# DeltaNet and SwiGLU FFN: diagonal blocks by substitution on VectorE, chunks in two half steps, output product behind each h tile

## The chip, the core and the metric

The kernel runs on one core of a Trainium2 chip. The metric is the device time of one execution in microseconds (us): 1305.42 as the median of three runs (1304.56 to 1309.9). The engines are TensorE (PE; PEld is its weight load), VectorE (DVE), ScalarE (ACT), GpSimd (POOL) and SyncE (SP), which issues the DMAs.

## What is computed

Four sequences of 768 tokens with 8 heads of width 48 go through a delta rule; its output, 3072 tokens of width 384, goes through a SwiGLU FFN of width 1536 behind an RMS norm. All is fp32; the FFN weights come as float64 and are converted in the kernel.

```python
k_n = k / (np.linalg.norm(k, axis=-1, keepdims=True) + 1e-06)
for t in range(S):
    y[:, :, t] = np.einsum('bhd,bhde->bhe', q[:, :, t], state)
    v_old = np.einsum('bhde,bhd->bhe', state, kt)
    state = state + bt[:, :, :, None] * np.einsum('bhd,bhe->bhde', kt, vt - v_old)
...
rms = np.sqrt(np.mean(x * x, axis=-1, keepdims=True) + 1e-06)
xn = x / rms * rms_g
g = xn @ w_gate
silu = g * (1.0 / (1.0 + np.exp(-g)))
val = xn @ w_val
return (silu * val @ w_out).astype(np.float32)
```

## The kernel before

Each sequence is cut into 6 chunks of 128 tokens; a unit n is chunk c = n // 4 of sequence b = n % 4, 24 units in all, with all 8 heads of the sequence. Within a chunk the recurrence is a triangular system with unit diagonal: (I + lower part of beta K K^T) u = beta (v - K state).

`invert(n)` (L249) prepares a unit. It normalizes k (knrm, krec), makes beta k (kb) and beta v, transposes k, beta k and q on PE (p_t, L285), and multiplies keys by keys and queries (p_g, L301, 64x128 tiles for even and odd heads); masks give xn (32x32 blocks on the diagonal) and gq (L309). Five doubling levels (L321) invert the four 32x32 diagonal blocks of each head: p_q (L326) and p_m (L337) are 32 matmuls of 32x32 each, with ScalarE (qc) and VectorE (new, m, mt) between. Then come ne (the inverse as block diagonal, POOL L358), the off-diagonal product (p_a L371, off) and xn = -ne off (p_x L384).

`recur(n)` (L391) uses it: r = beta v - beta K state (p_b), z0 = inverse r (p_z), three Horner steps u = z0 + xn u (p_h, L417), the output p_y from state and u, the state update p_s, the RMS norm (ms, rs, y) and the transposed FFN input xt.

`ffn(m)` (L490) takes two units, 256 tokens: for 12 tiles f of the hidden width p_gv (gate and value, L498), sil on ScalarE and h_f on VectorE; all 12 h_f are kept, and then the output product p_o (L516) runs over them for each half of the tokens.

`weights()` (L183) converts the weights in 30 items: seven VectorE operations on the two words of each float64 and a product on POOL (L243). All gate and value items come ahead of the output weights.

Every engine works through its queue in order. The order in which work is recorded comes from a plan (L534): each generator has a start time and a step, and the one that is due next is taken. Invert, recur and ffn of neighbouring units are so laid into one another; the build then puts each engine's instructions into a fixed order.

## Time and profile before

| | us |
|---|---|
| median of three runs | 1305.4 |
| profiled execution | 1309.4 |
| its span, first to last instruction | 1307.6 |
| mean granted TensorE clock | 0.97 of full |
| first p_gv of the FFN | 189.7 |

The page gives an engine's busy time and share, 40 equal slices with a digit of tenths for each, and the chain of work that ended last by engine and line. A row of a group has line, engine, operation, output<-inputs, shapes and count; behind the bar its busy time in all, the mean of one in ns, the idle time of the engine ahead of it and what ended that. Timeline rows begin with start and length in us. In PE rows 64*128 stands for the rows and columns of the tile, and 128x256 behind it for the output.

### The profile page before, as it was taken

The numbers are of one execution on the slowest core, as the hardware profiler recorded it, in microseconds if no ns is written. First come the engines' busy times: TensorE is split into PE (matmuls) and PEld (weight loads), VectorE is DVE, ScalarE is ACT, GpSimd is POOL, SyncE is SP. The second block draws the span as 40 slices with busy tenths as digits, with TensorE's granted clock in tenths as the row PEclk, the third lists the DMA queues.
The fourth block names the chain that finished last, engine by engine and source line by source line (L and its number), as shares of the span: only waits on it lengthen the run. The fifth ranks groups of instructions, "written<-read, shape, count | busy, mean of one in ns | idle before, by whom it ended". The sixth has DMA issues, their size and how long they took to land.

```text
span 1307.6 us, 43286 instructions
## 1 busy us (share of the span) xinstructions
PE 1222.7 (94%) x20206; PEld 1006.6 (77%) x20206; DVE 528.5 (40%) x1290; ACT 225.4 (17%) x506; POOL 216.6 (17%) x182
## 2 busy tenths in 40 slices
PE   3367898999999999999999999999999999999999
PEld 2266877878878878968878868878878878878976
DVE  6999763423333324334334333333432432332210
ACT  1011121112212212212212112112112121111110
POOL 6343341101111111011011011111111110000000
PEclk9967598999999999999999999999999999999999
DMA  8343210001000000010010010010000000000000
GB/s 149 111 121 98 72 30 14 14 21 20 14 21 15 19 21 14 14 27 14 15 27 14 9 28 19 9 26 20 9 20 15 15 14 8 3 8 8 1 13 13
DMA packets 83283, 35.91 MB, mean 27 GB/s; under 512 B 76160, under 2 KB 79232, under 8 KB 83104
## 3 DMA queue, kind: packets, MB, share of 16 engines
q1 hardware_dynamic: 83104, 33.14, 10.6%
q8 instruction: 159, 2.61, 0.8%
q14 instruction: 20, 0.16, 0.0%
HBM read 28.41 MB, written 4.72 MB: 25 GB/s over the span
## 4 chain that ended last, share of the span: by engine, by line
PE 76%; DVE 6%; POOL 3%; DMA 0%; issue 0%; ACT 0%; SPq 0%
PE p_gv L498 28%; PE p_o L516 13%; PE p_h L417 8%; PE p_q L326 5%; PE p_m L337 4%; PE p_x L384 3%; PE p_y L433 3%; PE p_z L409 3%; PE p_t L285 2%; POOL knrm L265 2%; PE p_a L371 2%; DVE xn L309 2%; PE p_y L424 1%; PE p_b L399 1%; DVE gq L309 1%; PE p_s L445 1%
## 5 line engine op out<-in xcount | busy, mean ns | idle before, releaser
L498 PE MATMUL p_gv<-xt,wg_sb 128*128 128x256 f32 x864 | 219.3, 389 | 0.0
L498 PE MATMUL p_gv<-xt,wv_sb 128*128 128x256 f32 x864 | 218.9, 389 | 0.0
L516 PE MATMUL p_o<-wo_sb,h_f 128*128 128x384 f32 x576 | 204.4, 497 | 0.0
L498 PEld LDWEIGHTS p_gv<-xt,wv_sb 128*128 128x128 f32 x864 | 155.4, 190 | 22.4 <-issue 3.3
L498 PEld LDWEIGHTS p_gv<-xt,wg_sb 128*128 128x128 f32 x864 | 153.8, 190 | 21.5 <-issue 3.3
L510 DVE TENSOR_TENSOR h_f<-sil,p_gv 128x256 f32<-128x256 f32 x144 | 60.2, 418 | 245.4 <-ACT sil L508 245.4
L516 PEld LDWEIGHTS p_o<-wo_sb,h_f 128*128 128x128 f32 x576 | 103.5, 190 | 65.1 <-issue 6.6
L418 DVE TENSOR_TENSOR u<-z,p_h 128x384 f32<-128x384 f32 x72 | 39.9, 554 | 216.5 <-PE p_h L417 216.5
L508 ACT ACTIVATE sil<-p_gv 128x256 f32<-128x256 f32 x144 | 55.3, 384 | 363.7 <-PE p_gv L498 363.7
L358 POOL TENSOR_TENSOR ne<-mt,mask_blk 128x1024 f32<-128x1024 f32 x24 | 57.5, 2395 | 312.6 <-DVE mt L354 276.4
L326 PEld LDWEIGHTS p_q<-m,xn 32*32 32x32 f32 x6144 | 65.5, 110 | 55.9 <-issue 53.4
L337 PE MATMUL p_m<-qc,mt 32*32 32x32 f32 x6144 | 78.0, 200 | 24.9 <-DVE mt L354 12.7
L417 PEld LDWEIGHTS p_h<-u,xn 128*128 128x128 f32 x768 | 98.1, 203 | 2.8 <-DVE u L418 1.1
L417 PE MATMUL p_h<-u,xn 128*128 128x48 f32 x768 | 98.2, 283 | 0.9 <-DVE u L418 0.9
L326 PE MATMUL p_q<-m,xn 32*32 32x32 f32 x6144 | 76.1, 199 | 20.8 <-DVE m L347 20.8
L337 PEld LDWEIGHTS p_m<-qc,mt 32*32 32x32 f32 x6144 | 66.3, 111 | 35.7 <-issue 24.6
L331 ACT COPY qc<-p_q 128x256 f32<-128x256 f32 x96 | 35.8, 372 | 312.6 <-PE p_q L326 312.6
L341 DVE TENSOR_TENSOR new<-p_m,mask_lev 128x256 f32<-128x256 f32 x96 | 40.6, 423 | 102.5 <-PE p_m L337 95.8
L301 PE MATMUL p_g<-kbq,knt 64*128 64x256 f32 x384 | 63.9, 412 | 1.4 <-ACT kbq L288 1.4
L276 POOL TENSOR_TENSOR v_raw<-v_raw,beta_t 128x384 f32<-128x384 f32 x24 | 20.8, 867 | 253.2 <-DMA v_raw<-in_v_dram 253.1
L472 POOL TENSOR_TENSOR rs<-ms,mhalf 128x1 f32<-128x1 f32 x24 | 13.4, 558 | 291.2 <-DVE ms L470 291.2
L384 PEld LDWEIGHTS p_x<-ne,off 128*128 128x128 f32 x384 | 54.2, 206 | 6.6 <-POOL ne L358 4.2
(102 smaller groups left out, 1386.3 us busy)
## 6 DMA issues: line engine op xcount, KB each, us to landing
kpad<-in_k_dram SPq DMA_DIRECT2D x24, 192.0 KB, 2.8
qpad<-in_q_dram SPq DMA_DIRECT2D x24, 192.0 KB, 2.8
v_raw<-in_v_dram SPq DMA_DIRECT2D x24, 192.0 KB, 2.8
raw<-in_moe_w_gate_dram SPq DMA_DIRECT2D x9, 512.0 KB, 4.4
raw<-in_moe_w_val_dram SPq DMA_DIRECT2D x9, 512.0 KB, 3.5
raw<-in_moe_w_out_dram SPq DMA_DIRECT2D x12, 384.0 KB, 3.1
out_dram<-o_sb SPq DMA_DIRECT2D x24, 192.0 KB, 1.9
beta_sb<-in_beta_dram SPq DMA_DIRECT2D x1, 96.0 KB, 2.1
```

The lines of the kernel that those rows point to most:

```text
L301: nc.tensor.matmul(p_gs[par][:, jj].rearrange("p a t -> p (a t)"), knt[lo : lo + DP, j], kbq[lo : lo + DP, j].rearrange("p a t -> p (a t)"),)
L326: nc.tensor.matmul(p_q[w, h], abd[w, h, w], m[w, h] if lev else ident_c[w], skip_group_check=True)
L337: nc.tensor.matmul(p_m[w, h], mt[w, h], qc[w, h], skip_group_check=True)
L341: nc.vector.tensor_tensor(out=new, in0=p_m, in1=mask_lev[:, lev, None, :].to_broadcast([128, H, W]), op=ALU.mult,)
L358: nc.gpsimd.tensor_tensor(out=ne, in0=mt[:, :, None, :].to_broadcast([128, H, NBLK, W]), in1=mask_blk[:, None].to_broadcast([128, H, NBLK, ...
L384: nc.tensor.matmul(p_x[:, i], off[:, h], ne_f[:, h])
L417: nc.tensor.matmul(p_h[:, h], xn[:, h], (u if it else z0)[:, h])
L418: nc.vector.tensor_tensor(out=u, in0=z0, in1=p_h, op=ALU.add)
L498: nc.tensor.matmul(p_gv[:, i], w_sb[:, t, f * 128 : (f + 1) * 128], xt[:, t], start=(t == 0), stop=(t == KT - 1),)
L508: nc.scalar.activation(out=sil, in_=p_gv[:, 0], func=ACTF.Silu)
L510: nc.vector.tensor_tensor(out=h_f, in0=sil, in1=p_gv[:, 1], op=ALU.mult)
L516: nc.tensor.matmul(p_o, hs[f][:, i * C : (i + 1) * C], wo_sb[:, f], start=(f == 0), stop=(f == FT - 1),)
```

## The change

Work is now planned by cycles of four units, chunk c of all four sequences, with two FFN calls in each cycle. `prepare(n)` forms key by key and key by query products in 64x64 tiles without beta (kqt, gp; p_g moves 192 columns). `invert(c)` inverts the diagonal blocks of all four units at once on VectorE: 128 partitions hold 4 blocks of 32 rows, the free dimension 32 heads by 32 by 32; 31 substitution steps of two operations update ttb. `merge(n)` joins 32-row blocks to 64-row ones (p_v, p_w) and makes x2 (p_x), which couples the two halves. `recur(n)` solves the upper 64 rows (p_z, u[lo]) and then the lower (p_z second, u[hi]); beta is applied to u. `weights()` now has 36 items of 384 columns, ordered so that three f tiles have gate, value and output weights together; ScalarE does four of the steps, and POOL none. In `ffn` the output product of tile f - 1 follows the gate and value product of tile f, in two PSUM buffers of its own.

```diff
-LEVELS = 5
-HORNER = C // W - 1
+HC = 64
+K1, K0, Q0, Q1 = 0, 2, 3, 4
...
+def weights(dt):
...
+                nc.scalar.activation(
+                    out=exp_f, in_=exp, func=ACTF.Relu, scale=1.0, bias=lift[:, 1:2]
+                )
+                nc.scalar.activation(
+                    out=exp_f, in_=exp_f, func=ACTF.Relu, scale=-1.0, bias=lift[:, 2:3]
+                )
...
-                nc.gpsimd.tensor_tensor(out=dst, in0=dst, in1=exp.bitcast(FP32), op=ALU.mult)
+                nc.vector.tensor_tensor(out=dst, in0=dst, in1=exp_f, op=ALU.mult)
...
+def prepare(n):
...
+                for par, i in ((0, 0), (1, 1), (0, 1), (1, 0)):
+                    lo = slice(DP * par, DP * (par + 1))
+                    rhs = pair[lo, K1 : K1 + 5 : 2] if i else pair[lo, K0 : K0 + 3]
+                    nc.tensor.matmul(
+                        p_gs[par][HC * i : HC * (i + 1), jj].rearrange("p (a t) -> p a t", a=3),
+                        pair[lo, K1 if i else K0],
+                        rhs,
+                        skip_group_check=True,
+                    )
...
+def invert(c, dt):
...
+            nc.vector.transpose(
+                out=gblk[p], in_=gp_all[p, :, o : o + W].rearrange("p x j -> p j x")
+            )
...
+        for i in range(W - 1):
+            n = W - 1 - i
+            shape = [128, n, i + 1]
...
+            nc.vector.scalar_tensor_tensor(
+                out=tmp,
+                in0=gblk[:, i, i + 1 :, None].to_broadcast(shape),
+                scalar=nbeta[:, c, i : i + 1],
+                in1=ttb[:, i : i + 1, 0 : i + 1].to_broadcast(shape),
+                op0=ALU.mult,
+                op1=ALU.mult,
+            )
+            to = ttb[:, i + 1 :, 0 : i + 1]
+            nc.vector.tensor_tensor(out=to, in0=to, in1=tmp, op=ALU.add)
+            yield dt
+        nc.vector.transpose(out=back, in_=ttb)
...
+def recur(n, dt):
...
+        for h in range(H):
+            for p in (lo, hi):
+                nc.tensor.matmul(
+                    p_z[p, h], tt[b][p, h], r[p, h], start=(h == 0), stop=(p is lo), skip_group_check=True
+                )
+        nc.vector.tensor_tensor(out=u[lo], in0=p_z[lo], in1=over_d(lo), op=ALU.mult)
...
+            nc.tensor.matmul(
+                p_z[hi, h], x2[:, h], u[lo, h], start=False, stop=True, skip_group_check=True
+            )
+        nc.vector.tensor_tensor(out=u[hi], in0=p_z[hi], in1=over_d(hi), op=ALU.mult)
...
+        for h in range(H):
+            first = c == 0 and h == 0
+            nc.tensor.matmul(
+                p_y[lo, h], sc[lo, h, HC : 2 * HC], u[lo, h], start=first, stop=True, skip_group_check=True
+            )
+            nc.tensor.matmul(
+                p_y[hi, h], sc[:, h, 2 * HC : 3 * HC], u[:, h], start=first, stop=True, skip_group_check=True
+            )
...
 def ffn(m):
...
+            if last is not None:
+                leave(f - 1, last)
+                yield 1
+            last = h_f
...
+    CYC = 3 * FT * B // 2
+    at(-69, weights(2.1))
+    for c in range(NCH):
+        t0 = CYC * (c - 1)
+        for b in range(B):
+            n = B * c + b
+            at(t0 - 1 + 5 * b, prepare(n))
+            at(t0 + 46 + 0.6 * b, merge(n, 2.7))
+            at(t0 + 50.1 + 2.7 * b, recur(n, 3))
+        at(t0 + 25.3, invert(c, 0.55))
+        for g in range(B // 2):
+            at(CYC * c + CYC // 2 * g, ffn(B // 2 * c + g))
```

Three places of the order. First PE, around the output of a unit in the steady stage, before:

```order
L498 MATMUL p_gv<-xt,wv_sb 128x256 x3
L424 MATMUL p_y<-state_95,kbq 128x96 x4
L433 MATMUL p_y<-u,gq 128x48 x8
L445 MATMUL p_s<-u,kpad_85 64x48 x8
L301 MATMUL p_g<-kbq,knt 128x256 x4
L516 MATMUL p_o<-wo_sb,h_f 128x384 x3
```

and of the change:

```order
L532 MATMUL p_gv<-xt,wg_sb 128x256 x3
L443 MATMUL p_s<-u,kpad_82 64x48 x8
L453 MATMUL p_y<-state_85,kqt_90 64x96 x8
L463 MATMUL p_y<-u,gp 64x48
L466 MATMUL p_y<-u,gp 64x48
L463 MATMUL p_y<-u,gp 64x48
L466 MATMUL p_y<-u,gp 64x48
```

The eight 128-row products of u became 16, in turn 64 rows (L463, upper half) and 128 rows (L466, lower half), one pair for each of the 8 heads (two pairs are shown).

Second VectorE, around the FFN's h_f, before:

```order
L341 TENSOR_TENSOR new<-p_m,mask_lev 128x256
L347 TENSOR_TENSOR m<-m,new 128x256
L354 STREAM_TRANSPOSE mt<-m 128x256
L510 TENSOR_TENSOR h_f<-sil,p_gv 128x256
L418 TENSOR_TENSOR u<-z_5648,p_h 128x384
```

and of the change, in the middle of the elimination (tmp and ttb are its product and its result):

```order
L543 TENSOR_TENSOR h_f<-sil,p_gv 128x256
L325 SCALAR_TENSOR_TENSOR tmp<-gblk,nbeta,ttb 128x156
L334 TENSOR_TENSOR ttb<-ttb,tmp 128x26x6
L325 SCALAR_TENSOR_TENSOR tmp<-gblk,nbeta,ttb 128x175
L334 TENSOR_TENSOR ttb<-ttb,tmp 128x25x7
L325 SCALAR_TENSOR_TENSOR tmp<-gblk,nbeta,ttb 128x192
L334 TENSOR_TENSOR ttb<-ttb,tmp 128x24x8
L325 SCALAR_TENSOR_TENSOR tmp<-gblk,nbeta,ttb 128x207
L334 TENSOR_TENSOR ttb<-ttb,tmp 128x23x9
L325 SCALAR_TENSOR_TENSOR tmp<-gblk,nbeta,ttb 128x220
L543 TENSOR_TENSOR h_f<-sil,p_gv 128x256
```

Between two h_f there now stand about nine operations of one dependent chain.

Third PE, where the first FFN call begins, before:

```order
L417 MATMUL p_h<-z_2081,xn 128x48 x6
L326 MATMUL p_q<-ident_c,xn 32x32 x12
L498 MATMUL p_gv<-xt,wg_sb 128x256 x2
L498 MATMUL p_gv<-xt,wv_sb 128x256 x3
L498 MATMUL p_gv<-xt,wg_sb 128x256 x2
L326 MATMUL p_q<-m,xn 32x32 x32
```

and of the change:

```order
L463 MATMUL p_y<-u,gp 64x48
L466 MATMUL p_y<-u,gp 64x48
L504 MATMUL p_xt<-ident,y 128x128 x3
L532 MATMUL p_gv<-xt,wg_sb 128x256 x3
L532 MATMUL p_gv<-xt,wv_sb 128x256 x3
L504 MATMUL p_xt<-ident,y 128x128 x3
L266 MATMUL p_t<-ident,qpad_83 128x128 x4
```

The first FFN call now stands behind the products of u and the state update of all four units of chunk 0; before, it stood among Horner steps and block inversions of units that were still under way.

## The prediction

> **What bounds the kernel now.** The page comes first: busy shares, the 40 slices, and the chain that ended last.

> ```profile
> PE 1222.7 (94%) x20206; PEld 1006.6 (77%) x20206; DVE 528.5 (40%) x1290; ACT 225.4 (17%) x506; POOL 216.6 (17%) x182
> ...
> PE   3367898999999999999999999999999999999999
> ...
> PEclk9967598999999999999999999999999999999999
> ...
> PE 76%; DVE 6%; POOL 3%; DMA 0%; issue 0%; ACT 0%; SPq 0%
> ```

> TensorE (PE) is the bound in all but the first six slices (some 200 us). The table of stages gives the two parts apart (busy us of each engine, then the clock, the DMA share, GB/s).

> ```profile
> 0.00:50.00 50.00, 15.49 (x418) 12.50 (x418) 38.93 (x111) 5.78 (x10) 27.88 (x28) 1.00 0.68 139
> 50.00:100.00 50.00, 30.06 (x764) 26.54 (x754) 46.53 (x97) 5.30 (x11) 18.28 (x12) 0.75 0.40 114
> 100.00:150.00 50.00, 39.08 (x882) 35.20 (x883) 44.81 (x108) 6.60 (x15) 17.62 (x15) 0.67 0.33 93
> ...
> 500.00:600.00 100.00, 98.58 (x1687) 80.78 (x1686) 35.42 (x88) 18.27 (x41) 14.24 (x12) 1.00 0.08 18
> ```

> At first VectorE (DVE) is busy 45 of 50 us while it converts weights, and PE waits. Later PE works 98.6 of 100 us at full clock and DVE 35. Third, the chain in order of time (start, length, what) gives the period.

> ```profile
> 189.74 1.80 PE p_gv L498 x4
> ...
> 424.30 2.79 PE p_gv L498 x12
> ...
> 525.53 2.79 PE p_gv L498 x12
> ...
> 1257.81 31.08 PE p_gv L498 x144
> 1288.89 15.49 PE p_o L516 x48
> ```

> One FFN call (256 tokens) alone takes 31.1 + 15.5 = 46.6 us: 216 ns for a p_gv record (256 columns move), 323 for p_o (384); a matmul in fp32 is two records. The period of one FFN and two chunks is 525.53 - 424.30 = 101.2 us, so two chunks cost 54.6 and four 109. A cycle of four chunks and two FFN calls takes 202 now.

> **What a small matmul costs.** The steady stage by instruction:

> ```profile
> 525.46 1.56 PE L498 MATMUL p_gv<-xt,wg_sb 128*128 128x256 f32 x6
> 526.86 1.46 PE L498 MATMUL p_gv<-xt,wv_sb 128*128 128x256 f32 x6
> 528.25 0.75 PE L326 MATMUL p_q<-m,xn 32*32 32x32 f32 x64
> 528.93 1.56 PE L498 MATMUL p_gv<-xt,wg_sb 128*128 128x256 f32 x6
> 530.33 1.88 PE L417 MATMUL p_h<-z,xn 128*128 128x48 f32 x16
> 532.14 0.75 PE L337 MATMUL p_m<-qc,mt 32*32 32x32 f32 x64
> ...
> 549.82 0.60 PE L285 MATMUL p_t<-ident,qpad 128*128 128x128 f32 x4
> 550.25 1.46 PE L498 MATMUL p_gv<-xt,wv_sb 128*128 128x256 f32 x6
> ...
> 554.25 0.67 PE L445 MATMUL p_s<-u,kpad 128*64 128x48 f32 x16
> 554.86 1.13 PE L301 MATMUL p_g<-kbq,knt 64*128 64x256 f32 x8
> 555.92 2.20 PE L516 MATMUL p_o<-wo_sb,h_f 128*128 128x384 f32 x6
> ```

> Start to start: p_h takes 1.81/16 = 113 ns a record, one switch of tile size in it; 107 without. Only 48 columns move, so its 128 weight columns set this: 0.84 ns a column, like the 216/256 of p_gv. The smaller tiles work side by side: p_g on two row halves takes (1.06 - 0.2)/8 = 108, half of 216; p_s on two column halves 32 to 38; p_q on four 32x32 tiles 0.68/64 = 10.6. A **switch** of tile size costs 0.10 us: the 12 p_gv records between p_m and p_q take 2.79 instead of 2.59, with one switch in and one out. So a record costs 0.84 ns times the wider of its weight and moving columns, divided by the tiles at work, and each change of tile size 0.10.

> **The new chunk work, per cycle of four chunks** (records; ns of one; stretches between FFN pieces at 0.2, p_g 0.3 for the fill):
> - transposes p_t 32 at 0.11 and p_xt 12 at 0.13: 5.0
> - p_g, 64x64, 192 columns move, four tiles: 128 x 40 + 8 stretches = 7.6
> - p_v, two tiles: 128 x 30 = 4.2; p_w, two: 128 x 16 = 2.6; p_x, one: 64 x 55 = 4.1
> - p_k, two, 96 columns move: 64 x 42 = 3.5; p_z first, two: 128 x 30 = 4.6; p_z second, one: 64 x 55 = 4.1
> - p_s as before, 2.8; p_y from the state, 64 x 42 = 2.9
> - p_y from u: 64 matmuls that **alternate** between 64 and 128 rows, each behind a switch. 0.10 + 2 x 0.055 + 0.02 for the first load = 0.23 each: 14.7. Without the switches 4.2. The nearest rows (p_gv to p_q, p_h to p_m above) change the tile and pay each time, so 14.7 is taken.

> Sum 56 in place of 109. What goes is p_q, p_m (nine pieces a chunk), p_h (three), p_a and the 128-row p_z and p_y. FFN stays at 93.1 and needs no switch, p_gv and p_o both being 128x128; that p_o follows each tile moves no PE time by itself.

> [...] p_v, p_w and p_z have two row tiles write one bank. [...]

> **The elimination on DVE.** Dependent operations of 256 elements, and the element rate:

> ```profile
> 576.90 0.42 DVE L341 TENSOR_TENSOR new<-p_m,mask_lev 128x256 f32<-128x256 f32 x1 [5.99 <-PE p_m L337]
> 577.36 0.43 DVE L347 TENSOR_TENSOR m<-m,new 128x256 f32<-128x256 f32 x1
> 577.83 0.45 DVE L354 STREAM_TRANSPOSE mt<-m 128x256 f32<-128x256 f32 x1
> ...
> L510 DVE TENSOR_TENSOR h_f<-sil,p_gv 128x256 f32<-128x256 f32 x144 | 60.2, 418 | 245.4 <-ACT sil L508 245.4
> ...
> L418 DVE TENSOR_TENSOR u<-z,p_h 128x384 f32<-128x384 f32 x72 | 39.9, 554 | 216.5 <-PE p_h L417 216.5
> ```

> 128 elements more cost 136 ns, 1.06 ns an element; 0.46 start to start leaves 0.19 fixed. Of 31 steps with two operations of (31 - i)(i + 1) elements: 62 x 0.19 + 10,912 x 1.06 ns = 23.4 us. Around them four transposes of 1024 (4 x 1.23) and a tail of two transposes, a product and two copies (5.9): 34 us a cycle. The other DVE work (24 h_f, 16 gp at 0.55, some 3.5 us a chunk for norms and recurrence) makes 34 + 10 + 9 + 14 = 67 of 150, so DVE is no bound on average.

> [...]

> But during the elimination PE has FFN work alone, and its h_f stand in DVE's queue between the steps. From the last p_g to p_v PE has eight f tiles, 8 x (2.59 + 1.29) = 31 us; DVE has 34 + 8 x 0.42 + two gp, 38.6. PE waits some 7.6 us a cycle there, at p_o for a late h_f and at p_v for tt. Two more for what the present stage also leaves idle (1.4%): 10. ScalarE's new wait (y behind rs of POOL) holds the silu behind it by about 1 us, four times, under 1.3 us p_gv pieces; I cost it at nothing, at most 4 us a cycle. The cycle: 93.1 + 56.1 + 10 = **159**.

> **The start.** One weight item now costs two tensor_scalar, two scalar_tensor_tensor and a tensor_tensor of 384, and ScalarE takes four operations.

> ```profile
> 24.40 0.43 DVE L209 TENSOR_SCALAR man<-raw 128x512 uint32<-128x512 uint32 x1
> ...
> 25.75 0.68 DVE L215 SCALAR_TENSOR_TENSOR wg_sb<-raw,wg_sb 128x512 f32<-128x512 uint32 x1
> 26.36 0.41 DVE L232 TENSOR_SCALAR exp<-exp 128x512 uint32<-128x512 uint32 x1
> ...
> L209 DVE TENSOR_SCALAR man<-raw 128x384 uint32<-128x384 uint32 x12 | 6.7, 558 | 0.0
> L215 DVE SCALAR_TENSOR_TENSOR wo_sb<-raw,wo_sb 128x384 f32<-128x384 uint32 x12 | 6.6, 547 | 0.0
> ...
> L463 ACT COPY y<-p_y 128x384 f32<-128x384 f32 x24 | 11.5, 479 | 50.8 <-PE p_y L433 50.8
> ```

> Starts lie 0.07 closer than durations (0.68 long, 0.61 apart): 0.47 for the three of 547 to 554. The tensor_scalar of 512 takes 0.43 near its beginning but the 384 ones 0.558 on average, beside POOL's products of L243, which are gone; I take 0.27, so 1.95 an item, 2.74 at most. ScalarE needs 4 x 0.48 = 1.9, hidden beside. In DVE's order 22 of 36 items stand ahead of the end of the first elimination. As now, the first weight operation can start at 24 us; up to the end of the elimination there are left 22 items (43), the elimination with its waits filled by weight operations (62 x 0.08 + 11.6 = 16.5), four transposes (4.9) and ten gp (4.7): 69 us of DVE work, and 5 for waits: 98. Then 4 for the tail, and PE must go through p_v to p_y of **all four** chunks, 38 us by the list above without p_k and the state's p_y. First p_gv at **140** (now 189.7). Ends: 17 more if the conversions stay slow, 19 more if the clock stays at the 0.67 of the third row; 10 less without the switches in p_y.

> **The sum.** 140 + 5 x 159 + the last two FFN calls 93.1 + 4.5 (last h_f, copy, output, as now about 3 behind the last p_o) = 1033 of span, now 1307.6. The profiled execution took 1309.4, so 1.8 lie around the span: 1035; the median shown is 4 under that execution: **1031**. DMA moves the same bytes at a share of 0.08; it is in no term.

> **Rivals.**
> 1. Alternating p_y doesn't drain, since both kinds lie on different columns: 10.5 less in each of six passes, 968. For it: p_s alternates column halves at 32 ns. Against: every change of rows in the trace pays.
> 2. The strided and broadcast operands of the elimination run slower, half as long again: 12 more a cycle, 1031 + 60 + 10 = 1101. No row shows such operands.
> 3. The start doesn't shorten, conversions and elimination queue as the weights do now and the first p_gv stays at 190: 1081.
> [...]
> 5. **Slower:** every hop between 64-wide tiles drains, like a switch. 352 matmuls a cycle besides p_y's 64 hop (p_g, p_v, p_w, p_k, p_z, p_s, state). At 0.23 each, 0.43 for p_g, they cost 94 instead of 28: 66 a cycle and 40 at the start, 1031 + 330 + 40 = 1401. It decides from 49 a cycle, 0.14 a hop. p_s and p_q hop without it.

> **Chances.** Forecast 0.52; rivals 0.20, 0.10, 0.08, 0.05, 0.04; nearly unchanged 0.01. The range takes in rivals 1 to 4 and the dearer start: 955 to 1115. A change of 0.5%, about the least that a measurement of this kernel can tell, leaves faster 0.95, same 0.01, slower 0.04.

> **What would show it.** First p_gv near 140; periods of 159 between FFN pairs; p_y from u near 3.7 us a chunk (rival 1: 1.1); a DVE stretch of 34 us with PE idle near p_v; p_g at 40 ns a record, p_z and p_v at 30. The forecast is wrong if DVE or ScalarE ends the waits throughout the cycle, or if p_z, p_v and p_g take twice their prices.

## The result and the profile after

The changed kernel takes 1130.09 us (median of 4 runs, 1124.92 to 1130.37), the kernel before beside it 1306.27: a ratio of 0.864, 95% interval 0.861 to 0.867. It is faster, as forecast, by 176 us and not by 275; the time lies 15 us above the range. The profiled execution took 1130.3, its span 1128.5. One execution of combo2 below, 1067.80 us, is over 1.5% longer than that kernel's fastest and is left out as a slow one.

The same lines of the page as before, of the changed kernel: busy shares, PE and its clock in 40 slices, and the chain that ended last.

```profile
PE 1006.1 (89%) x8142; PEld 773.5 (69%) x8142; DVE 485.6 (43%) x1116; ACT 275.8 (24%) x590; POOL 83.3 (7%) x97
...
PE   5202997989999989999989999989999989999998
...
PEclk9555559998979996998998989998999998978999
...
PE 70%; DVE 21%; ACT 4%; issue 1%; POOL 1%; POOLq 0%; ACTq 0%
```

PE still bounds the steady stage. New is the third row: before, the clock digit was 9 from the eighth slice to the end; now digits of 6 to 8 come back in every cycle, in slices where PE is busy. The chain's 21% on DVE runs through the elimination, which ends just ahead of PE's short waits at p_v. The windows table cut at the starts of the FFN pairs gives the size (busy us of each engine, then clock, DMA share, GB/s). Row one is the start from the first p_v to the first p_gv, then come the five cycles and the last two FFN calls.

```profile
103.80:165.00 61.20, 60.31 (x714) 53.04 (x715) 25.73 (x59) 25.97 (x55) 2.85 (x5) 0.50 0.28 72
165.00:354.20 189.20, 175.51 (x1392) 133.09 (x1392) 88.34 (x207) 49.39 (x106) 23.57 (x23) 0.88 0.10 24
354.20:526.30 172.10, 166.25 (x1389) 127.09 (x1388) 69.94 (x155) 32.92 (x75) 13.22 (x14) 0.91 0.09 19
526.30:696.10 169.80, 163.02 (x1390) 124.93 (x1389) 70.03 (x155) 32.86 (x75) 13.22 (x14) 0.94 0.09 20
696.10:861.90 165.80, 160.19 (x1389) 122.86 (x1388) 69.15 (x151) 32.40 (x73) 10.74 (x12) 0.95 0.08 19
861.90:1031.80 169.90, 163.88 (x1326) 125.67 (x1325) 63.35 (x131) 31.20 (x71) 2.18 (x4) 0.92 0.03 8
1031.80:1128.50 96.70, 93.25 (x385) 72.73 (x383) 10.11 (x24) 11.61 (x29) 0.00 (x0) 0.99 0.04 13
```

The forecast had 140 for the first p_gv, 159 for each cycle, 97.6 for the end. Measured: 165.0 (25 more), cycles that are together 71.8 longer, 96.7 (1 less). That is the whole excess of the span, some 96. Length times what the clock lacks, row by row over the five cycles (189.2 x 0.12, 172.1 x 0.09 and so on), gives 70.3 us, and the start ran at 0.50 from end to end. So the excess of the cycles has about the size of what the clock took. That is only a sum; the experiments must show it.

Where the clock falls in a cycle, by PE's timeline of the changed kernel (start, length, what; in brackets the wait ahead):

```profile
430.89 0.59 PE L532 MATMUL p_gv<-xt,wg_sb 128*128 128x256 f32 x2
433.08 0.41 PE L366 MATMUL p_v<-tt,gp 32*64 32x32 f32 x4 [1.60 <-ACT tt L340]
433.42 1.29 PE L532 MATMUL p_gv<-xt,wg_sb 128*128 128x256 f32 x4
435.06 7.03 PE L366 MATMUL p_v<-tt,gp 32*64 32x32 f32 x124 [0.35 <-ACT tt L340]
442.02 2.93 PE L532 MATMUL p_gv<-xt,wv_sb 128*128 128x256 f32 x6
...
515.62 0.31 PE L463 MATMUL p_y<-u,gp 64*64 64x48 f32 x2
515.86 0.32 PE L466 MATMUL p_y<-u,gp 128*64 128x48 f32 x2
...
516.83 0.45 PE L463 MATMUL p_y<-u,gp 64*64 64x48 f32 x2
517.20 0.45 PE L466 MATMUL p_y<-u,gp 128*64 128x48 f32 x2
517.58 2.93 PE L532 MATMUL p_gv<-xt,wg_sb 128*128 128x256 f32 x6
```

Six p_gv records take 2.93 us here instead of 1.46, p_v 57 ns a record, an alternating p_y 0.376 us a matmul and just before 0.244. The halved clock shows in the length of full FFN records, though their shapes are the same. In this cycle the trace's records of the granted clock name three halved stretches (start and length in us):

```
434.3 20.5   (p_v, p_w)      485.5 3.4   (p_y)      516.2 6.8   (p_y)
```

All halved stretches of the steady stage last 3.4 us or a multiple of it.

### The profile page after: what moved, and what is told of

Same layout as the page of the kernel before. It is cut to its first block, busy times and chain, and to the rows that moved or that the text cites. A ratio compares the mean times of both kernels' runs of the same rounds, so it can differ in the third digit from the quotient of the medians.

```text
span 1128.5 us, 18814 instructions
## 1 busy us (share of the span) xinstructions
PE 1006.1 (89%) x8142; PEld 773.5 (69%) x8142; DVE 485.6 (43%) x1116; ACT 275.8 (24%) x590; POOL 83.3 (7%) x97
## 4 chain that ended last, share of the span: by engine, by line
PE 70%; DVE 21%; ACT 4%; issue 1%; POOL 1%; POOLq 0%; ACTq 0%
PE p_gv L532 27%; PE p_o L519 12%; DVE tmp L325 6%; DVE ttb L334 5%; PE p_y L466 5%; PE p_y L463 5%; DVE gblk L316 4%; PE p_v L366 4%; PE p_g L293 3%; PE p_x L388 2%; PE p_z L425 2%; PE p_z L433 2%; PE p_w L379 2%; ACT tt L340 2%; PE p_k L413 1%; DVE h_f L543 1%
## 5 line engine op out<-in xcount | busy, mean ns | idle before, releaser
L366 PE MATMUL p_v<-tt,gp 32*64 32x32 f32 x768 | 44.6, 285 | 74.7 <-ACT tt L340 74.7
L366 PEld LDWEIGHTS p_v<-tt,gp 32*64 32x64 f32 x768 | 43.1, 207 | 79.6 <-ACT tt L340 79.6
L325 DVE SCALAR_TENSOR_TENSOR tmp<-gblk,nbeta,ttb 128x31 f32<-128x31 f32 (+15 forms) x186 | 74.3, 399 | 4.6
L300 DVE TENSOR_TENSOR gp<-p_g,mask 128x384 f32<-128x384 f32 x96 | 49.2, 551 | 52.5 <-PE p_g L293 52.5
L466 PE MATMUL p_y<-u,gp 128*64 128x48 f32 x384 | 66.3, 259 | 0.0
L334 DVE TENSOR_TENSOR ttb<-ttb,tmp 128x31 f32<-128x31 f32 (+15 forms) x186 | 63.5, 341 | 5.0
L463 PE MATMUL p_y<-u,gp 64*64 64x48 f32 x384 | 65.2, 254 | 0.0
L293 PE MATMUL p_g<-kqt 64*64 64x192 f32 x768 | 51.6, 365 | 12.8 <-DVE gp L300 6.5
L466 PEld LDWEIGHTS p_y<-u,gp 128*64 128x64 f32 x384 | 40.8, 150 | 11.9
L463 PEld LDWEIGHTS p_y<-u,gp 64*64 64x64 f32 x384 | 40.0, 146 | 13.0
L316 DVE STREAM_TRANSPOSE gblk<-gp 32x1024 f32<-32x1024 f32 x24 | 46.2, 1926 | 0.5
```

The lines of the kernel that those rows point to most:

```text
L293: nc.tensor.matmul(p_gs[par][HC * i : HC * (i + 1), jj].rearrange("p (a t) -> p a t", a=3), pair[lo, K1 if i else K0], rhs, skip_group_che ...
L300: nc.vector.tensor_tensor(out=gp[b][:, 4 * g + par : 4 * g + 4 : 2], in0=p_gs[par], in1=mask[:, None, :].to_broadcast([128, 2, 3 * HC]), o ...
L316: nc.vector.transpose(out=gblk[p], in_=gp_all[p, :, o : o + W].rearrange("p x j -> p j x"))
L325: nc.vector.scalar_tensor_tensor(out=tmp, in0=gblk[:, i, i + 1 :, None].to_broadcast(shape), scalar=nbeta[:, c, i : i + 1], in1=ttb[:, i : ...
L334: nc.vector.tensor_tensor(out=to, in0=to, in1=tmp, op=ALU.add)
L366: nc.tensor.matmul(p_v[HC * (a // 2) : HC * (a // 2 + 1), h], gp[b][w, h, 0:HC], tt[b][w, h, W:HC], skip_group_check=True,)
```

## The experiments

Two theories. **T1, thin work:** the clock is halved when a stretch of 3.4 us holds little work of the array, also while PE shows busy. **T2, waits:** it is halved only by PE's waits (for the elimination at p_v, at p_o, in the start). The gate, below, is whatever grants PE its clock. Medians below; the kernel before ran beside each, at 1307 to 1310. "Halved time" is the sum of the halved stretches after 170 us in the profiled execution: 139.9 for the changed kernel. Work at half clock takes up to twice as long (six p_gv records 2.93 us for 1.46, an alternating p_y 0.376 for 0.244), so by an estimate up to half of the halved time is lost.

### Sorted output products (py_order)

```diff
             nc.tensor.matmul(
                 p_y[lo, h], sc[lo, h, HC : 2 * HC], u[lo, h], start=first, stop=True, skip_group_check=True
             )
+        for h in range(H):
+            first = c == 0 and h == 0
             nc.tensor.matmul(
                 p_y[hi, h], sc[:, h, 2 * HC : 3 * HC], u[:, h], start=first, stop=True, skip_group_check=True
             )
```

> The eight upper products of p_y from u (64 rows) come first and then the eight lower ones (128 rows), so a unit has 2 switches of tile size there in place of 16. At full clock a pair costs 2 x 0.244 us with switches; without, some 2 x 0.06, so the 16 records groups shrink from about 3.9 us to about 1.2 with the two switches left: 2.7 us a unit less at full clock, more where the clock is halved, of which the part outside the throttled stretches counts. Theory T1 (the clock is halved in windows in which small or draining tiles do little array work, also while PE shows busy): the half-clock stretches in the output products go with the alternation too, 24 units x 2.7 = 65 plus some of the 20 us that these stretches lose, a time of about 1055 to 1070. Theory T2 (the clock is halved only by PE's waits): 24 x 2 to 2.7 less, the half-clock stretches stay where they are, 1070 to 1085. Should alternation not be what costs (rival: the hop itself, whatever the order), no change, 1125 to 1130.

1059.69 us (1058.89 to 1061.19): 70 less, by one loop split in two. Halved time 87.9. The stretches at p_y are gone, those that begin at p_v stay (10.2 to 20.5 us in each steady cycle). The sorted products of one unit at full clock:

```profile
453.71 1.13 PE L463 MATMUL p_y<-u,gp 64*64 64x48 f32 x16
454.77 1.13 PE L468 MATMUL p_y<-u,gp 128*64 128x48 f32 x16
455.83 1.56 PE L534 MATMUL p_gv<-xt,wv_sb 128*128 128x256 f32 x6
```

They take 455.83 - 453.71 = 2.12 us; in turn, 16 matmuls at 0.244 took 3.90. So the order itself is worth 1.78 us a unit, 43 over 24 units, and not the 2.7 and 65 of the expectation. Half of the 52 us of halved time that went is 26, and 43 + 26 = 69 is near the 70 gained. The time lies in T1's range. T2 gave 1070 to 1085 with the price of the expectation; with the measured price it would give some 1087.

### Merge in four stretches (spread)

```diff
-            at(t0 + 46 + 0.6 * b, merge(n, 2.7))
+            at(t0 + 46 + 2.7 * b, merge(n, 2.7))
```

> The merge of the four units starts 2.7 plan steps apart in place of 0.6, so that the 64 p_v records come as four stretches of 16 with FFN pieces between; the wait for the elimination ahead of the first stays. T1 (thin tiles): the halved stretch at the merge (20.5 us from 434.3 in the steady stage of the profile after) shrinks to under half, 6 to 10 us a cycle less, about 1095 to 1110. T2 (waits): the halved stretch starts as before behind the same wait and is as long, 1125 to 1135.

1126.28 us (1122.99 to 1137.31), no gain that can be told, as T2's range has it: T1's number missed. Yet the halved stretch behind the first p_v of the second cycle went from 20.5 to 3.4 us; new ones came at the alternating p_y (24 us between 470 and 515). Halved time fell to 102.4. The time alone would have spoken for T2, the clock records do not.

### A shorter elimination (short_elim)

```diff
         for i in range(W - 1):
+            if 8 <= i < 20:
+                continue
```

> Leaves out elimination steps 8 to 19 of 31 (the inverse is then wrong for these columns; nothing else changes). VectorE needs some 11 us a cycle less, so PE should not wait ahead of p_v nor at p_o for h_f. T2 (waits halve the clock): the halved stretches that begin at p_v vanish, 10 to 20 us a cycle less and 5 to 8 of waits, some 1000 to 1040 in all, with 11 to 20 less at the start. T1 (thin tiles): halved stretches at p_v, p_y and p_s stay at about their lengths; only waits go (5 to 8 a cycle) and 11 to 20 at the start: 1070 to 1095.

1078.84 us, in T1's range. But the halved stretch at p_v is all but gone in four of five cycles (clock 0.98, 0.96, 0.96 and 0.95 from the second cycle on, for 0.91, 0.94, 0.95 and 0.92 in the changed kernel), as T2 says; and as p_v starts earlier, FFN pieces now stand between its parts (17, 15 and 32 matmuls), so the run changes both suspects. The stretches at p_y and p_s stay, behind no wait; the clock still lacks 0.02 to 0.05. Not decided by this run.

### PE kept busy in the start (warm)

```diff
                 nc.vector.tensor_tensor(out=dst, in0=dst, in1=exp_f, op=ALU.mult)
+                if 12 <= i < 23:
+                    p_d = ps_delta([128, WT], "p_d")
+                    for _ in range(4):
+                        nc.tensor.matmul(p_d, ident, dst, skip_group_check=True)
```

> Adds 4 products of 128x128 by 384 columns, of no use, behind each of the weight items 12 to 22, so that PE is at work in the 50 us in which it was idle; the output is the same. Clock theory of the start (the 61 us from the first p_v to the first p_gv are the forecast's 38 at half clock): p_v to p_gv takes 40 to 48, the first p_gv comes at 145 to 152 in place of 165, about 1110 to 1117. Rival (VectorE's and ScalarE's latencies in the chain p_v to p_y set it): first p_gv stays within 5 us of 165, 1125 to 1135.

1126.95 us, first p_gv at 164.4: both numbers lie in the rival's ranges, not in those of the clock theory. The windows of this kernel from the first p_v to the first p_gv:

```profile
103.80:114.50 10.70, 10.70 (x90) 7.20 (x92) 7.99 (x17) 7.28 (x12) 0.00 (x0) 0.50 0.16 47
114.50:138.40 23.90, 23.90 (x468) 20.13 (x469) 12.23 (x31) 16.64 (x36) 1.11 (x2) 1.00 0.52 131
138.40:164.40 26.00, 26.00 (x193) 20.61 (x187) 7.47 (x18) 3.31 (x8) 2.13 (x3) 0.50 0.21 47
```

The timeline rows of the added products that fell into it:

```profile
104.31 1.65 PE L241 MATMUL p_d<-wg_sb,ident 128*128 128x384 f32 x2
...
109.44 4.21 PE L241 MATMUL p_d<-wg_sb,ident 128*128 128x384 f32 x6
...
116.98 2.85 PE L241 MATMUL p_d<-wv_sb,ident 128*128 128x384 f32 x8
...
122.60 2.85 PE L241 MATMUL p_d<-wv_sb,ident 128*128 128x384 f32 x8
```

These 24 records lie in the path itself and take 11.3 us by the starts of the rows behind them. Without them the stage is 49 long and not 61, with 18 of it at full clock. PE is busy all the while, so PE did not stand waiting for DVE or ScalarE: the rival falls by its reason, and the stage is PE work at the clock it gets. How long it would be at full clock throughout, this run does not show. Near the end it fell back to 0.50 with PE busy 26.00 of 26.00.

### The gate alone (micro)

```python
for cols in (32, 40, 48, 56, 64):
    seg(f"p_full{cols}", [(a, a)], cols, 190)
seg("p_alt", [(lo, lo), (a, hi)], 48, 168)
seg("p_sorted_lo", [(lo, lo)], 48, 380)
seg("p_sorted_hi", [(a, hi)], 48, 380)
seg("p_z", [(lo, lo), (hi, hi)], 48, 580)
seg("p_v", [((32, 64), lo), ((96, 128), hi)], 32, 700)
seg("p_s", [(a, lo), (a, hi)], 48, 640)
```

Each pair is the tile's rows and columns, then columns moved and count.

> Computes nothing of the kernel (the output is zeros): PE alone runs eleven stretches of one kind of small product, each some 40 us long, with 31 us of dense 128x128 products of 384 columns ahead of each; every operand lies ready, so PE never waits. Work of a stretch = rows x columns of the tile / 16,384, times columns moved x 0.84 ns, over the time of a record: full tiles that move 32, 40, 48, 56, 64 columns 0.25, 0.31, 0.38, 0.44, 0.50; p_alt (64 and 128 rows in turn) 0.12; sorted 64 rows 0.18, sorted 128 rows 0.37; p_z 0.33; p_v 0.11; p_s 0.67. T1 (the clock follows the array's work in windows of 3.4 us, with a threshold between the 0.28 and 0.37 that the traces so far give): half clock in p_full32, p_alt, sorted 64 rows and p_v from the first or second window on, full clock in p_full56, p_full64 and p_s, the rest near the edge. T2 (only waits halve the clock): full clock in all eleven.

The windows table of micro, cut at the stretches, from the full tiles that move 48 columns on, in the order of the code:

```profile
253.10:329.40 76.30, 76.30 (x381) 76.29 (x380) 0.00 (x0) 0.00 (x0) 0.53 0.00 1
362.40:404.70 42.30, 42.30 (x381) 42.30 (x380) 0.00 (x0) 0.00 (x0) 1.00 0.00 1
435.80:478.10 42.30, 42.30 (x381) 42.30 (x380) 0.00 (x0) 0.00 (x0) 1.00 0.00 1
509.20:569.80 60.60, 60.60 (x337) 46.05 (x336) 0.00 (x0) 0.00 (x0) 0.54 0.00 1
602.10:679.90 77.80, 77.80 (x761) 77.67 (x760) 0.00 (x0) 0.00 (x0) 0.53 0.01 1
713.50:758.00 44.50, 44.50 (x762) 44.44 (x761) 0.00 (x0) 0.00 (x0) 1.00 0.01 2
789.10:823.10 34.00, 34.00 (x1162) 33.92 (x1161) 0.00 (x0) 0.00 (x0) 1.00 0.02 4
854.20:925.20 71.00, 71.00 (x1402) 70.89 (x1401) 0.00 (x0) 0.00 (x0) 0.53 0.01 3
959.00:996.50 37.50, 37.50 (x1281) 37.41 (x1281) 0.00 (x0) 0.00 (x0) 1.00 0.02 4
```

This decides it: thin work alone halves the clock. PE is busy 100% in all eleven stretches and never waits; six run at half clock (mean 0.53 or 0.54; 32 and 40 columns, not shown, take 76.20 and 76.30 us at 0.53, as 48), five at full (1.00). T2 as the only cause falls; that waits do it too is not excluded here. Which measure sorts them? A full-tile record takes 42.3/380 = 111 ns at full clock; 48 columns are 48 x 0.84/111 = 0.36 of it, 56 are 0.42. Rows times columns of the tile, the measure of the expectation, does not sort: p_z has 0.25 x 48 x 0.84 over 29 ns = 0.35 and runs at full. **Rows times columns moved** (rows / 128 x columns moved x 0.84 ns, over the time of a record; the share, below) does: p_alt 0.25 and p_v 0.23 (by the records of the kernel at full clock, 122 and 29 ns), one 64-row tile 0.35 (at the 58 ns of the sorted 128-row ones), against p_z 0.69, the sorted 128 rows 0.69, p_s 1.38. Halved up to 0.36, full from 0.42. All operands were the same few values; whether values matter was not tested.

### Spread and sorted (combo, combo2)

combo has the two edits above; combo2 also this, so that FFN pieces stand between the state's products and the two halves of p_y:

```diff
+        yield dt / 3
         for h in range(H):
             first = c == 0 and h == 0
             nc.tensor.matmul(
                 p_y[lo, h], sc[lo, h, HC : 2 * HC], u[lo, h], start=first, stop=True, skip_group_check=True
             )
+        yield dt / 3
...
-        yield dt + 1
+        yield dt / 3 + 1
```

> The sorted p_y of py_order and the spread merge together; the wait ahead of p_v stays. T1: the halved stretch of 10 to 20 us a cycle at the merge that py_order still has shrinks to under 7, 3 to 6 us a cycle less, less 0.5 for some five more switches: 1035 to 1050. T2: the halved stretches stay behind the same waits, 1055 to 1065 as in py_order.

> As combo, with the state's products, the upper and the lower products of p_y recorded one plan step apart, so that FFN pieces stand between them. T1: no window of the output products falls under the edge, at most one or two halved windows a cycle, mean clock behind the first p_gv above 0.97, 1025 to 1045. T2: as py_order and combo, 1055 to 1065.

1054.87 us (1053.04 to 1057.20), 0.807 of before (0.804 to 0.809), and 1060.01 (1051.40 to 1062.99), 0.809 (0.804 to 0.813): T1's numbers missed (T2's fit combo2, and combo lies at their edge), and combo2 no better than combo. Yet combo's halved time is 54.6, for py_order's 87.9. A halved stretch of 10.2 us still begins behind PE's waits ahead of p_v in two cycles of combo (1.62 and 0.62 us in one, 1.22 and 0.61 in the other), though FFN records stand inside; in the other three, waits of 1.2 and 0.6 bring none there. What decides between them is not shown.

### A wider p_v (wide_v, combo_w)

On py_order and on combo:

```diff
-        p_v = ps_delta([128, H, W], "p_v")
+        p_v = ps_delta([128, H, HC], "p_v")
...
-                    tt[b][w, h, W:HC],
+                    tt[b][w, h],
...
-        nc.scalar.copy(vs, p_v)
+        nc.scalar.copy(vs, p_v[:, :, W:HC])
```

> py_order with p_v moving 64 columns of tt in place of 32; the 32 more are not read by anything, and the weight load of 64 columns should already take as long, so that a p_v record should cost the same. The share of rows times columns moved doubles, 0.25 to 0.5, over the edge of 0.38 to 0.42 that the stretches of micro show. T1, with the edge on rows times columns moved: p_v no longer holds the clock at half, so the halved stretch at the merge (10 to 20 us in py_order) shrinks to what p_w and the wait ahead of p_v bring, 3 to 10 us, and the useless work makes the kernel 2 to 5 us a cycle faster: 1035 to 1053. T2, or an edge on rows times columns of the tile (p_v then 0.25): halved stretches as in py_order, 1057 to 1063.

> combo with the same wide p_v. T1: two or three of the remaining halved windows of a cycle go, 1038 to 1052 against 1054.9. T2: 1053 to 1058.

1051.29 us (0.803 of before, 0.801 to 0.805; py_order 0.810, 0.808 to 0.812) and 1059.42 (0.808, as combo). The first lies in T1's range, but not for T1's reason: halved time is 84.6, near py_order's 87.9. The gain came once: the second FFN call starts at 222.8 for 232.3, and in the first py_order waits 5.0 us at p_g where this kernel does not. combo_w lies above both ranges: the wider p_v brings nothing there. PE's timeline of wide_v at the merge:

```profile
399.56 0.44 PE L366 MATMUL p_v<-tt,gp 32*64 32x64 f32 x4 [1.60 <-ACT tt L340]
399.93 1.79 PE L534 MATMUL p_gv<-xt,wg_sb 128*128 128x256 f32 x4
401.65 7.08 PE L366 MATMUL p_v<-tt,gp 32*64 32x64 f32 x124
```

7.08 us for 124 records: twice the columns at no cost, and the clock half already when they start. At half clock the same records do half as much per time (57 ns each here; those of 32 columns take 57 at half clock and 29 at full). That suggested, and did not show, that a halved stretch holds itself.

### Entered at half clock (micro2)

```diff
     def seg(name, tiles, cols, n):
         dense(48)
-        p = psum.tile([128, 512], FP32, name=name, tag="b", bufs=2)
-        for k in range(n):
-            (r0, r1), (c0, c1) = tiles[k % len(tiles)]
+        for w, c, m in (("p_thin", 32, 100), (name, cols, n)):
+            p = psum.tile([128, 512], FP32, name=w, tag="b", bufs=2)
+            for k in range(m):
+                (r0, r1), (c0, c1) = tiles[k % len(tiles)] if w == name else (a, a)
```

> As micro, but behind the dense products of each stretch stand 100 products of full tiles that move 32 columns (share 0.25, they halve the clock), and the stretch under test follows them. Theory L (the gate counts rows times columns moved per time, so at half clock every share counts half, against the same edge of 0.38 to 0.42): full tiles that move 64 columns (0.48, now 0.24) and 96 (0.72, now 0.36), the sorted 128-row products (0.69, now 0.35) and p_z (0.69, now 0.35) stay at half clock for the whole stretch, though 64 columns, the sorted ones and p_z ran at full clock in micro; full tiles that move 128 (1.0, now 0.5) and p_s (1.38, now 0.69) come back to full within two windows. Rival (a fixed edge on what the tile would do at full clock): all six come back to full.

The windows of micro2 at the stretches of full tiles with 64 and with 96 columns, and of p_z:

```profile
72.50:153.60 81.10, 81.10 (x382) 81.10 (x382) 0.00 (x0) 0.00 (x0) 0.50 0.00 1
224.40:269.30 44.90, 44.90 (x382) 44.90 (x382) 0.00 (x0) 0.00 (x0) 0.94 0.00 1
...
568.80:605.20 36.40, 36.40 (x1161) 36.38 (x1160) 0.00 (x0) 0.00 (x0) 0.92 0.02 4
```

The stretch with 64 columns took 42.3 us behind dense work and takes 81.1 behind thin work, the same instructions: it holds itself at half clock to its end. 96 columns, the sorted 128 rows and p_z (0.69 to 0.73 at full, about 0.35 at half) come back within two windows of 3.4 us (clock 0.94, 0.95 and 0.92 over the stretch), against theory L, as do 128 columns and p_s (0.96 each). So in these stretches the edge on the way up is lower per time (between 0.24 and 0.35) than on the way down; 64 columns (0.48 at full) stay where they were, 0.69 lifts itself. By rows times columns of the tile p_z would be at 0.17 here and 64 columns at 0.24, the wrong way round.

### Merge and recurrence later (combo_wl, combo_l), and the fourth corner (alt_wl)

```diff
-            at(t0 + 46 + 2.7 * b, merge(n, 2.7))
-            at(t0 + 50.1 + 2.7 * b, recur(n, 3))
+            at(t0 + 48.5 + 2.7 * b, merge(n, 2.7))
+            at(t0 + 52.6 + 2.7 * b, recur(n, 3))
```

combo_wl is combo_w with it, combo_l is combo with it, and alt_wl is combo_wl with p_y in turn again.

> combo_w with merge and recur 2.5 plan steps later, so that FFN pieces stand where PE waited for the end of the elimination ahead of p_v. The waits of 1 to 2 us at p_v and the low window they make go too: both theories expect fewer halved windows; T1 1030 to 1045, with the halved time behind the first p_gv under 40 us. Rival: the output of the chunk comes 3 us later and the next cycle's PE waits elsewhere, 1050 to 1060.

> combo_wl with p_v moving 32 columns as in the change. If the FFN work that now stands around each p_v stretch is what holds the clock, the width does not matter: 1030 to 1038. If the width did it, halved stretches of 7 to 10 us a cycle come back at the merge: 1045 to 1055.

> combo_wl with the upper and lower products of p_y in turn, as the change records them. The 16 switches a unit come back at 0.44 us a pair more or less at full clock: 63 us, 1096 where the clock stays full. T1: the products in turn (share 0.31 in micro) and the p_s beside them halve the clock again, as in spread, so 1098 to 1115, and no halved stretch at the merge. Were the merge stage the whole cause of the halved time: 1090 to 1098.

combo_wl 1033.38 us (1032.66 to 1034.09; 0.789 of before, 0.788 to 0.790), combo_l 1035.32 (0.792, 0.790 to 0.795), alt_wl 1105.71 (1092.66 to 1108.07; 0.844, 0.839 to 0.849). The windows of combo_wl by cycle:

```profile
320.60:474.40 153.80, 148.89 (x1390) 115.38 (x1389) 70.29 (x156) 32.94 (x75) 13.20 (x14) 0.99 0.10 22
474.40:628.10 153.70, 148.76 (x1389) 115.36 (x1388) 70.18 (x156) 32.87 (x74) 13.20 (x14) 0.99 0.10 22
628.10:782.00 153.90, 148.96 (x1389) 115.25 (x1388) 69.94 (x155) 32.71 (x74) 13.19 (x14) 0.99 0.09 20
```

Clock 0.99, halved time 19.3 us in all, one window of 3.4 a cycle. FFN pieces now stand where PE waited longest for tt, and around each p_v. The wide p_v is worth some 2 to 4 us here, so the later start did most of it. In alt_wl a single window of 3.4 us is left at the merge in two of the cycles, none in the others, and those at p_y stand, as T1 has it.

The windows that combo_wl still has are due to waits. That of the second cycle starts at 382.1; PE's rows there:

```profile
381.95 2.78 PE L521 MATMUL p_o<-wo_sb,h_f 128*128 128x384 f32 x4 [2.46 <-DVE h_f L545]
384.52 1.97 PE L534 MATMUL p_gv<-xt,wg_sb 128*128 128x256 f32 x6
```

The wait of 2.46 us stands among dense records only, and the four p_o records behind it take 2.78 instead of 1.45. The other windows too begin at such waits (three of 2.5 us at p_o, and one of 3.7 at p_g in the first cycle). So a wait of 2.46 us brings a halved window here, as thin work does: T1 holds, and T2 holds for a part. The four corners, each as a ratio to the kernel before:

| | merge as in the change | spread and later |
|---|---|---|
| p_y in turn | 0.864 | 0.844 |
| p_y sorted | 0.810 | 0.789 |

Sorting p_y is worth 0.054 to 0.055, some 70 us, the merge 0.020 to 0.022, 26 to 28 us, whichever is done first. combo_wl beats both kernels.

The five cycles of each profiled execution, parted by the clock records (us; the clock's share is half of the halved time in them, an estimate):

| | length | clock's share | rest |
|---|---|---|---|
| the change | 866.8 | 69.8 | 797.0 |
| spread | 857.5 | 52.9 | 804.6 |
| alt_wl | 841.8 | 41.6 | 800.2 |
| py_order | 806.9 | 43.6 | 763.3 |
| combo | 798.2 | 28.5 | 769.7 |
| combo_l | 778.0 | 14.2 | 763.8 |
| combo_wl | 775.5 | 9.5 | 766.0 |

Sorting takes 34 us off the rest, near the 36 that 1.78 us a unit make in 20 units, and 26 to 32 off the clock's share. The later, spread merge takes 28 to 34 off the clock's share and adds 3 to the rest. The spread merge alone takes 15 to 17 off the clock's share but adds 6 to 8 to the rest, which is most of why its time hardly moved.

## Why the prediction was wrong

**The step that failed** is the clock. The forecast took every price from rows of the steady stage before, where the clock is 1.00, and summed them for a stage made of other work; "PE must go through p_v to p_y of all four chunks, 38 us" and "The cycle: 93.1 + 56.1 + 10 = 159" have no clock term. The runs showed in its place a loss to the clock of some 69.8 (by the table above) of the 71.8 us by which the five cycles are longer, and a start at clock 0.50 from the first p_v to the first p_gv. Only for the start was a slow clock named, as a dear end of 19, and for a clock of 0.67. The gate answers to the work that the change itself put in: before, thin 32x32 products stood between dense p_gv records (64 p_q records of 0.75 us in all between p_gv stretches of 1.46 and 1.56, clock 1.00); the merge lays 64 p_v matmuls at a share of 0.23 in a row, right behind a wait (1.60 and 0.35 us), and p_y in turn is at 0.25.

No idle time is needed for the clock to fall: micro's six thin stretches are halved with PE busy throughout (48 columns: 76.30 of 76.30 us at 0.53). Nor does busy time bring the clock back: at the merge 124 p_v records run for 7.03 us, over two windows of 3.4, without a wait, and take 57 ns each (29 at full clock).

Point by point:

- **Start.** Elimination and its tail were to end at 102; the first p_v stands at 103.8. The stage behind it took 61.2 at clock 0.50. Half of it is 31, and not all of it halves (p_y in turn takes 0.376 us at half clock and 0.244 at full), so at full clock it would come near the forecast's 38, by estimate. First p_gv 165.0 for 140.
- **Cycles.** 172.1, 169.8, 165.8 and 169.9 less the clock's share (15.5, 10.2, 8.3, 13.6) leave 156 to 160: 159 was about right for full clock, in part by luck, as PE idles some 4 us less than summed and works some 4 more. The first cycle, 189.2, also has weight conversions and a wait of 5.0 us at p_g for gp. combo_wl's 153.8 with sorted p_y is 5 above the forecast's 159 - 10.5, with waits 5 lower (153.80 - 148.89 for 10): some 10 us of work are more than summed. Of these, 4.3 are the sorted p_y, 1.6 p_w and 1.7 the halved window; the rest may be the switches of its many short stretches, which was not counted out.
- **Prices at full clock, start to start.** p_z 31 ns (30), p_x 58 (55), p_k 45 (42), p_s 32, p_y in turn 0.244 us a matmul (0.23), a stretch of 16 p_g records 0.81 us (0.94). Two terms were mis-sized: p_w takes 29 ns for 16, 1.6 us a cycle, and p_y without the switches 4 x 2.12 = 8.5 us for 4.2. The 4.2 lets upper and lower products work side by side, at 33 ns a record; sorted, a record takes 58. So the 10.5 of rival 1 is 7.1 as a price of the order.
- **Waits.** 10 a cycle forecast; by the windows PE idles 5.6 to 6.8. The list of PE's waits names the forecast's places:

```profile
PE p_v L366 <- ACT tt L340: 74.7, 12, 64.6
PE p_o L519 <- DVE h_f L543: 23.1, 13, 2.5
```

Without the 64.6 of the start, that is 10 us at p_v and 23 at p_o over the kernel (in all, times, longest).

- **DVE** (groups: busy, mean ns):

```profile
L316 DVE STREAM_TRANSPOSE gblk<-gp 32x1024 f32<-32x1024 f32 x24 | 46.2, 1926 | 0.5
L336 DVE STREAM_TRANSPOSE back<-ttb 128x1024 f32<-128x1024 f32 x6 | 7.5, 1243 | 0.2
L325 DVE SCALAR_TENSOR_TENSOR tmp<-gblk,nbeta,ttb 128x255 f32<-128x255 f32 x12 | 5.8, 480 | 0.2
L334 DVE TENSOR_TENSOR ttb<-ttb,tmp 128x255 f32<-128x255 f32 x12 | 5.1, 424 | 0.3
```

From the first transpose to the last copy of tt it takes 40.7 us in the second cycle (395.2 to 435.9), h_f included; 38.6 was forecast. Rival 2 holds only for the strided reads: the transposes from gp take 1.93 for 1.24, 2.7 us a cycle. A step's product with broadcast operands takes 480 ns for 255 elements and the sum behind it 424: dearer at most by an eighth, not by half.
- **Rivals 1 and 5** fall. A matmul of 64 and 128 rows in turn costs 0.244 us, and sorting it saved 43 us by that price and 26 by the clock; hops between equal tiles cost nothing like a switch (p_s 32 ns a record). No run shows two row tiles on one bank in each other's way: p_z, which writes so, takes 31 ns a record and p_v 29. Rival 3 gave a late first p_gv; it came late (165.0), by another cause.

**Open:** whether rows times columns moved is the gate's own measure or only sorts these eleven stretches; how far the start would shorten with dense work beside it, since there is no FFN work yet to lay between. At the merge thin work and waits are not parted: short_elim and the later start changed both. Nor is it shown why the spread merge adds 6 to 8 us to the rest of the cycles and the later one only 3.

## What to carry to other kernels

Busy time does not keep the clock (0.53 in micro with PE busy 76.30 of 76.30 us): add up rows times columns moved per 3.4 us (the measure that sorts the stretches here, halved up to 0.36 and full from 0.42), and where thin products must run, lay dense ones between them rather than run them in a block right behind a wait (spreading the merge and starting it later took 28 to 34 us off the clock's share here). When a change replaces broad work by thin work, price it at half clock first (p_v took 57 ns a record for 29), and read the clock column of the windows before the busy one. Sort products by tile shape; the order that alternates paid 1.78 us for 14 more changes here, 0.13 each.
